# Moving a few sums and the gate weighting to other engines in a convolution plus mixture-of-experts kernel

## The chip, the core and the metric

The kernel runs on one core of one Trainium2 chip. Its time is the device time of one execution in microseconds (us), given as the median of several runs. The core has a matmul engine (TensorE, PE in the profile, with its weight loads as PEld) and three engines for elementwise work: VectorE (DVE), ScalarE (ACT) and GpSimd (POOL). SyncE (SP) issues nearly all DMA transfers; GpSimd issues the scatters with indices.

## The reference, cut to what matters

Each of 8 sequences of 5696 rows and 128 columns is convolved along its length with one common filter, and the result goes row by row through a mixture of experts, in which each row uses one expert of eight.

```python
Yf = np.fft.rfft(x, n=2 * S, axis=1) * np.fft.rfft(h, n=2 * S, axis=0)[None]
x = np.fft.irfft(Yf, n=2 * S, axis=1)[:, :S, :].reshape(B * S, D)

logits = x @ w_gate
expert_idx = np.argmax(logits, axis=1)
probs = softmax(logits)
gate_w = probs[np.arange(N), expert_idx]
for e in range(8):
    mask = expert_idx == e
    out[mask] = gate_w[mask, None] * (np.maximum(x[mask] @ w1[e], 0.0) @ w2[e])
```

Here B = 8, S = 5696, D = 128, N = B * S = 45568; w1 is 128x1024 and w2 1024x128 for each expert.

## The kernel before, in words

The long transform is split into a 119-point and a 48-point part. The batches go through it in three groups of 2, 3 and 3 (`SPLIT`). For each group there is an opening 119-point stage (`phase_a`), a 48-point stage (`phase_b`) and a closing 119-point stage with gating and sorting (`phase_c`). The opening stage of group 1 and of group 2 runs as a guest inside the closing stage of the group before.

**The 48-point stage.** In groups 1 and 2 it works on 120 items of 384 columns, software-pipelined by fixed lags. One item is: `forward` (matmuls into `xp`, L528), `product` (three VectorE instructions L540, L545 and L547 that read `xp` from PSUM and write `zt` and `xs`), `combine` (the sum `zt + xs`, L555), `inverse` (matmuls into `vp`, L564) and `save` (a ScalarE copy, L579). With the lags (1, 2, 4, 5), `combine` of an item is issued one item step after its `product`, and `inverse` two item steps after `combine`. `combine` runs on GpSimd, except that the first `ALONE[g]` items of group g run on VectorE; `ALONE` is (0, 0, 20), so that these are the first 20 items of group 2, in the third 48-point stage.

**The sort.** The closing stage finds an expert and a place for each row, and appends to the list `sorts`. `sort_one` takes one entry off the list and issues one scatter on GpSimd (L656) into the sorted rows `SR`, and a short filler instruction behind it (L650). The scatters are spread over the steps; what is left on the list when the closing stage ends is issued one by one in the next stage, one in each expert step, from inside `relu`.

**The experts.** Rows are read back in sorted tiles of 256 (182 of them). A tile has four steps; a step is `layer1` (matmuls L1164 into `mh`), `relu` on ScalarE (L1170) with the rest of the fp32 split on VectorE (L1172), and `layer2` (matmuls L1185 into `ma`) two steps later. In the step k = 2 TensorE also transposes the finished tile before it and the rows of the next one into one PSUM bank `mx` (L183); ScalarE and VectorE then cut the new rows in two parts (`xtb`, L1154 and L1155), ScalarE copies a finished sum out (`ot`, L1195), and `emit` multiplies the finished rows by their gate weights (L1203) and writes them over `xr`. `deliver` issues the scatters to `out` (L1240), two for each tile, on GpSimd. While a closing stage runs, finished tiles are stored to a staging buffer instead (`leave`, L1216), and read back later.

**The order.** Everything is issued in an order that is worked out when the program is built: `run` takes, of the streams that are alive, the one with the least planned time. So the interleaving of expert steps and transform work does not react to what happens on the chip. Each engine works its own queue in order. The experts run beside the second 48-point stage, both later closing stages and the third 48-point stage, and then alone to the end.

Of the kernel before, what the change touches and what calls it, by code (L numbers as in the profile page):

```python
# [17 lines left out]
AF = mybir.ActivationFunctionType  # L18
ALU = mybir.AluOpType
# [23 lines left out]
LD = 4  # L43
SHARES = (0.39, 0.93, 0.998, 0.84)
AHEAD = 2
ALONE = (0, 0, 20)
HALVES = ((12,), (8, 24), (24,))
STEP = 1420
MIX_A = (0.0, 0.45, 0.8)
# [28 lines left out]
def conv_moe(ctx: ExitStack, tc: tile.TileContext, I, out, B, S, D, E, F, split):  # L78
    nc = tc.nc
    P = 128  # L80
# [373 lines left out]
    def phase_b(gr, guest=None):  # L454
        g, cb, cw, nch, QB, QW = gr.g, gr.cb, gr.cw, gr.nch, gr.qb, gr.qw
# [95 lines left out]

        def combine(n):
            zt, xs = zts[n]
            eng = nc.vector if n < ALONE[g] else nc.gpsimd
            eng.tensor_tensor(out=zt, in0=zt, in1=xs, op=ALU.add)  # L555

        def inverse(n):
# [43 lines left out]
        for n in range(N + ds_ + 2 + (HOLD if QW == 1 else 0)):  # L601
# [21 lines left out]
            if 0 <= n - dc < N:  # L623
                combine(n - dc)
# [18 lines left out]
    sorts = []  # L643
# [556 lines left out]

    def emit(t, count):
        op, xr = obank.pop(t), rows.pop(t)
        nc.vector.tensor_tensor(  # L1203
            out=xr[:, :, :D], in0=op, in1=xr[:, :, D : D + 1].broadcast_to([P, 2, D]), op=ALU.mult
        )
        if state["defer"] and slot[0] < STAGED:
            leaving.append((count, STG[slot[0]], xr))
            slot[0] += 1
        else:
            pending.append((xr, 0))  # L1210
            pending.append((xr, 1))
# [52 lines left out]
    def pipeline(lo, hi):  # L1264
# [3 lines left out]
        while True:  # L1268
# [57 lines left out]
            if to is not None:  # L1326
                emit(to, len(hist))
# [141 lines left out]
```

## Time and profile before

| what | value |
|---|---|
| median of 3 runs | 2147.75 us (2144.11 to 2147.92) |
| the profiled execution's own time | 2146.88 us |
| its span, first to last instruction | 2145.2 us |
| busy share of the span: TensorE, VectorE, ScalarE, GpSimd | 96%, 73%, 51%, 59% |
| mean granted TensorE clock | 0.989 of full speed |

The busy share of an engine is a mean over stages that differ. A TensorE that is busy is not a TensorE at its best, since the ends of its matmuls are modelled. The shares for VectorE, ScalarE and GpSimd can be read as they stand.

### The profile page before, as it was taken

Reading aid. Unit: us, or ns where it says so; the run is one execution under the profiler, and the core shown is the slowest. Engines: PE = TensorE matmul, PEld = TensorE weight load, DVE = VectorE, ACT = ScalarE, POOL = GpSimd, SP = SyncE. Lnnn points to the kernel's source line nnn. Section 1 sums busy time; section 2 is a strip of 40 time slices with the busy share of each in tenths; the row PEclk is TensorE's granted clock in tenths of the full one; section 3 lists DMA queues with packets and bytes.
Section 4 is the critical chain, followed back from the end, with each engine's and each line's share of the span. In section 5 each row is a group of like instructions: output and inputs, shape, how many; then the busy total and the mean of one; then the engine's idle time right before and its main releaser. Section 6 shows DMA issues by size and latency. Waiting matters only on the chain.

```text
span 2145.2 us, 47047 instructions
## 1 busy us (share of the span) xinstructions
PE 2052.4 (96%) x14284; PEld 1763.9 (82%) x14284; DVE 1556.4 (73%) x3731; ACT 1104.5 (51%) x2359; POOL 1264.6 (59%) x1399
## 2 busy tenths in 40 slices
PE   7899899899999999989999999999999999999998
PEld 5788666666667988876777779999989999999998
DVE  3598856699987788879988885777765555555554
ACT  5688755233334666633443345655544444554544
POOL 5366547565653388882665661788876444444443
PEclk9999999999999999999999999999999999999999
DMA  9899999799997788767889886666645543444441
GB/s 340 291 301 325 320 395 366 213 278 279 272 279 234 288 273 296 264 198 218 250 249 248 243 246 228 212 209 211 199 149 186 170 139 108 142 138 143 143 144 34
DMA packets 236901, 494.39 MB, mean 230 GB/s; under 512 B 33553, under 2 KB 146446, under 8 KB 236647
## 3 DMA queue, kind: packets, MB, share of 16 engines
q1 hardware_dynamic: 212279, 443.06, 66.2%
q0 software_dynamic: 24368, 48.29, 6.9%
q8 instruction: 116, 1.90, 0.4%
q14 instruction: 138, 1.13, 0.2%
HBM read 598.31 MB, written 176.80 MB: 361 GB/s over the span
## 4 chain that ended last, share of the span: by engine, by line
PE 29%; issue 15%; POOL 13%; DMA 6%; DVE 6%; ACT 1%; SPq 1%; POOLq 1%; DVEq 0%; ACTq 0%
PE mh L1164 9%; PE ma L1185 8%; POOL out L1240 8%; POOL SR L656 3%; PE vp L564 3%; PE xp L528 3%; PE yp L742 2%; DMA SR<-rt,pi 2%; DMA wb<-WD 2%; POOL c_fcs L650 1%; PE mx L183 1%; DVE hs L1172 1%; PE pa L315 1%; PE tp L183 1%; DMA vq<-VU 1%
## 5 line engine op out<-in xcount | busy, mean ns | idle before, releaser
L1172 DVE SCALAR_TENSOR_TENSOR hs<-mh,hs 128x512 fp32r<-128x512 f32 x728 | 501.4, 691 | 371.6 <-ACT hs L1170 366.5
L1164 PE MATMUL mh<-xtb,wb 128*128 128x256 f32 x4368 | 686.0, 293 | 27.2 <-DMA wb<-WD 12.7
L1170 ACT ACTIVATE hs<-mh 128x512 fp32r<-128x512 f32 x728 | 435.7, 599 | 449.3 <-PE mh L1164 435.4
L1164 PEld LDWEIGHTS mh<-xtb,wb 128*128 128x128 f32 x4368 | 582.8, 189 | 95.3 <-issue 34.3
L1185 PE MATMUL ma<-hs,wb 128*128 128x256 f32 x4368 | 653.7, 285 | 7.3 <-DMA wb<-WD 7.3
L1185 PEld LDWEIGHTS ma<-hs,wb 128*128 128x128 f32 x4368 | 566.9, 190 | 8.7 <-DMA wb<-WD 8.7
L656 POOL DMA_INDIRECT SR<-rt,pi x384 | 402.8, 1049 | 196.3 <-issue 55.0
L1240 POOL DMA_INDIRECT out<-xr x250 | 243.8, 975 | 316.0 <-DVE xr L1203 257.7
L555 POOL TENSOR_TENSOR zt<-zt,xs 128x384 f32<-128x384 f32 (+1 forms) x280 | 298.3, 1075 | 115.3 <-DVE xs L547 86.9
L579 ACT COPY vt<-vp 96x384 f32<-96x384 f32 (+1 forms) x300 | 149.1, 497 | 349.2 <-PE vp L564 344.4
L564 PE MATMUL vp<-zt,mi 128*96 128x384 f32 (+1 forms) x720 | 259.2, 455 | 7.2 <-DVE xs L547 5.8
L528 PE MATMUL xp<-uq,mt 96*128 96x384 f32 (+1 forms) x720 | 258.7, 454 | 4.4 <-ACT vt L579 2.3
L540 DVE TENSOR_TENSOR zt<-xp,hh 128x384 f32<-128x384 f32 (+1 forms) x300 | 174.0, 580 | 54.6 <-PE xp L528 40.6
L564 PEld LDWEIGHTS vp<-zt,mi 128*96 128x96 f32 x720 | 113.3, 163 | 100.2 <-issue 52.1
L1240 POOL DMA_INDIRECT out<-xb x114 | 111.1, 975 | 135.3 <-ACT hs L1170 111.0
L547 DVE SCALAR_TENSOR_TENSOR xs<-xp,hh 64x384 f32<-64x384 f32 (+1 forms) x300 | 175.7, 586 | 6.1
L545 DVE TENSOR_TENSOR xs<-xp,hh 64x384 f32<-64x384 f32 (+1 forms) x300 | 173.2, 577 | 6.0
L315 PE MATMUL pa<-xc,fcr 120*128 120x512 f32 x576 | 166.8, 420 | 11.0 <-ACT xc L293 4.0
L528 PEld LDWEIGHTS xp<-uq,mt 96*128 96x128 f32 x720 | 121.7, 192 | 34.7 <-issue 13.1
L315 PEld LDWEIGHTS pa<-xc,fcr 120*128 120x128 f32 x576 | 101.5, 192 | 44.5 <-DVE rk L867 7.5
L650 POOL TENSOR_TENSOR c_fcs<-c_fcs 120x64 f32<-120x64 f32 (+1 forms) x288 | 125.9, 437 | 6.2
L742 PE MATMUL yp<-vr,gcr 120*120 120x384 f32 x576 | 117.5, 338 | 1.2 <-DVE vr L730 1.1
(137 smaller groups left out, 2275.6 us busy)
## 6 DMA issues: line engine op xcount, KB each, us to landing
wb<-WD SPq DMA_DIRECT2D x728, 512.0 KB
vq<-VU SPq DMA_DIRECT2D x64, 768.0 KB
VU<-ut SPq DMA_DIRECT2D x48, 768.0 KB
uq<-VU SPq DMA_DIRECT2D x60, 576.0 KB
VU<-vt SPq DMA_DIRECT2D x60, 576.0 KB
xt<-x SPq DMA_DIRECT2D x96, 256.0 KB
xr<-SR SPq DMA_DIRECT2D x182, 130.0 KB
hh<-HS SPq DMA_DIRECT2D x120, 192.0 KB
```

Source lines behind the costliest of these rows:

```text
L315: done = nc.tensor.matmul(banks[m], lhs, rhs, start=(k == 0), stop=(k == len(ops) - 1))
L528: nc.tensor.matmul(xj, mt[:, k0 + j, :], uc.rearrange("p (b d) -> p b d", d=D), start=True, stop=True)
L540: nc.vector.tensor_tensor(out=zt, in0=x3, in1=hv[:, 0].broadcast_to([P] + wide), op=ALU.mult)
L547: nc.vector.scalar_tensor_tensor(out=xs[to], in0=x3[at], scalar=-1.0, in1=him, op0=ALU.mult, op1=ALU.mult)
L555: eng.tensor_tensor(out=zt, in0=zt, in1=xs, op=ALU.add)
L564: nc.tensor.matmul(vp[:K2, j * cw : (j + 1) * cw].rearrange("p (b d) -> p b d", d=D), mi[:, k0 + j, :], zt.rearrange("p b (j d) -> p b j d ...
L656: s = nc.gpsimd.indirect_dma_start(out=SR[:, :], out_offset=IndirectOffsetOnAxis(ap=pi[:, b : b + 1], axis=0), in_=rt[:, b, :], in_offset= ...
L1164: nc.tensor.matmul(hp[:, u, :], wb[:, a, f, :], xt[:, b, :], start=(n == 0), stop=(n == 2))
L1170: done = nc.scalar.activation(hs[:, 0], hp, AF.Relu)
L1172: nc.vector.scalar_tensor_tensor(out=hs[:, 1], in0=hp, scalar=0.0, in1=hs[:, 0].bitcast(F32), op0=ALU.max, op1=ALU.subtract)
L1185: nc.tensor.matmul(accs[t], wb[:, a, f, :], hs[:, b, u, :], start=(k == 0 and u == 0 and n == 0), stop=(k == NPAIR - 1 and u == 1 and n == 2),
L1240: sc = nc.gpsimd.indirect_dma_start(out=out[:, :], out_offset=IndirectOffsetOnAxis(ap=xr[:, s, D + 1 : D + 2].bitcast(I32), axis=0), in_=x ...
```

## The change

Two edits. In `combine` the engine of the sum is no longer chosen by the number of the item: in group 2 it is VectorE as long as the list `sorts` is not empty at the time of issue, and GpSimd from then on. In `emit` the product of a 128x256 PSUM tile with the gate weights, one VectorE instruction, becomes two ScalarE activations of 128x128 with the gate weight as a scale for each partition.

```diff
-ALONE = (0, 0, 20)
...
         def combine(n):
             zt, xs = zts[n]
-            eng = nc.vector if n < ALONE[g] else nc.gpsimd
+            eng = nc.vector if g == 2 and sorts else nc.gpsimd
             eng.tensor_tensor(out=zt, in0=zt, in1=xs, op=ALU.add)
...
     def emit(t, count):
         op, xr = obank.pop(t), rows.pop(t)
-        nc.vector.tensor_tensor(
-            out=xr[:, :, :D], in0=op, in1=xr[:, :, D : D + 1].broadcast_to([P, 2, D]), op=ALU.mult
-        )
+        for s in range(2):
+            nc.scalar.activation(xr[:, s, :D], op[:, s], AF.Copy, scale=xr[:, s, D : D + 1])
```

## Rows read from the trace of the kernel before

**Rows 1.** Windows by stage: PE, PEld, DVE, ACT, POOL busy (count), clock, DMA share, GB/s.
```profile
415.00:655.00 240.00, 229.66 (x1098) 153.76 (x1096) 224.62 (x412) 83.33 (x186) 149.54 (x149) 0.99 1.02 272
655.00:955.00 300.00, 285.37 (x2137) 253.63 (x2137) 238.31 (x787) 183.60 (x423) 213.03 (x287) 0.98 0.79 261
955.00:1022.00 67.00, 61.96 (x350) 44.84 (x350) 64.65 (x131) 23.87 (x49) 20.24 (x27) 1.00 0.76 208
1022.00:1290.00 268.00, 261.91 (x1513) 201.34 (x1512) 232.15 (x426) 110.25 (x228) 163.62 (x165) 0.99 0.89 250
1290.00:1600.00 310.00, 300.87 (x2546) 286.31 (x2545) 224.24 (x752) 178.26 (x417) 219.20 (x285) 0.99 0.64 203
1600.00:2146.00 546.00, 535.70 (x4579) 534.60 (x4578) 301.97 (x528) 266.20 (x528) 259.37 (x275) 1.00 0.41 134
```

**Rows 2.** Waits of DVE in 415 to 655 us: total us, times, longest.
```profile
DVE zt L540 <- PE xp L528: 7.4, 7, 2.6
```

**Rows 3.** Windows 978 to 1022 us of all engines, columns as in rows 1.
```profile
978.00:1022.00 44.00, 40.83 (x224) 28.78 (x224) 42.52 (x79) 16.43 (x35) 8.69 (x9) 1.00 0.79 220
```

**Rows 4.** Waits of PE in 955 to 1022 us.
```profile
PE mh L1164 <- DVE hs L1172: 3.6, 5, 1.5
```

**Rows 5.** Instructions of line L555 on DVE over the span.
```profile
L555 DVE TENSOR_TENSOR zt<-zt,xs x20: 557/559/634, 963.4 to 1019.9; 128x384 f32<-128x384 f32 x20
```

**Rows 6.** Timeline of POOL: the last sort scatter and what follows.
```profile
975.09 1.01 POOL L656 DMA_INDIRECT SR<-rt,pi  x1 [1.69 <-ACT hs L1170]
...
986.22 0.99 POOL L1240 DMA_INDIRECT out<-xr  x1 [9.79 <-DVE xr L1203]
```

**Rows 7.** Timeline of ACT: the relu ahead of that scatter.
```profile
974.19 0.60 ACT L1170 ACTIVATE hs<-mh 128x512 fp32r<-128x512 f32 x1 [0.67 <-PE mh L1164]
```

**Rows 8.** Timeline of DVE in the early third 48-point stage.
```profile
975.22 0.56 DVE L555 TENSOR_TENSOR zt<-zt,xs 128x384 f32<-128x384 f32 x1
975.81 0.69 DVE L1172 SCALAR_TENSOR_TENSOR hs<-mh,hs 128x512 fp32r<-128x512 f32 x1
...
985.52 0.41 DVE L1203 TENSOR_TENSOR xr<-mx,xr 128x256 f32<-128x256 f32 x1
985.86 0.55 DVE L540 TENSOR_TENSOR zt<-xp,hh 128x384 f32<-128x384 f32 x1
```

**Rows 9.** Windows of line L540 (one instruction for each item): DVE busy (count).
```profile
978.00:1022.00 44.00, 8.23 (x15) 1.00 0.79 220
1022.00:1290.00 268.00, 54.02 (x98) 0.99 0.89 250
```

**Rows 10.** Windows of line L1203 by stage: DVE busy (count).
```profile
415.00:655.00 240.00, 5.40 (x13) 0.99 1.02 272
655.00:955.00 300.00, 8.30 (x20) 0.98 0.79 261
955.00:1022.00 67.00, 2.08 (x5) 1.00 0.76 208
1022.00:1290.00 268.00, 9.13 (x22) 0.99 0.89 250
1290.00:1600.00 310.00, 13.72 (x33) 0.99 0.64 203
1600.00:2146.00 546.00, 37.02 (x89) 1.00 0.41 134
```

**Rows 11.** Groups by line and shape: busy us, mean ns | idle before, releaser.
```profile
L555 POOL TENSOR_TENSOR zt<-zt,xs 128x384 f32<-128x384 f32 x220 | 222.2, 1020 | 81.2 <-DVE xs L547 69.9 <-PE vp L564 7.8 <-PE ma L1185 2.2
L1195 ACT COPY ot<-ma 128x256 f32<-128x256 f32 x182 | 67.8, 373 | 17.0 <-PE ma L1185 3.0
L797 ACT COPY lt<-tp 96x120 f32<-96x120 f32 x64 | 17.8, 279 | 0.0
```

**Rows 12.** Timeline of ACT: the relu behind an emit, with the idle time before it.
```profile
1434.26 0.60 ACT L1170 ACTIVATE hs<-mh 128x512 fp32r<-128x512 f32 x1 [0.58 <-PE mh L1164]
...
1705.28 0.60 ACT L1170 ACTIVATE hs<-mh 128x512 fp32r<-128x512 f32 x1 [1.00 <-PE mh L1164]
```

**Rows 13.** Waits of PE in 1290 to 1600 us.
```profile
PE mh L1164 <- DVE hs L1172: 6.3, 10, 3.0
PE mh L1164 <- ACT hs L1170: 1.4, 4, 0.5
```

## The prediction, made before the change was run

> **What bounds the kernel now.** I read the windows by stage first, since the kernel is a chain of stages with different limits [rows 1]. Expert work begins with the second 48-point stage, and nothing of the change acts before it. Five stretches remain, and one for the start of the third 48-point stage.
>
> In the second 48-point stage (415 to 655 us) VectorE is busy 224.62 of 240 us, and its list of waits holds one entry of size, 7.4 us for TensorE [rows 1, 2]. The reader is to see that VectorE hardly ever waits: it sets the pace. The same row shows the DMA engines at a share of 1.02, so a second limit lies close behind. At the start of the third 48-point stage VectorE is fuller still: 42.52 of 44 us in 978 to 1022 us [rows 3]. There TensorE waits for it, 3.6 us of it at the first layer for a free `mh` bank [rows 4]. After 1022 us TensorE is busy 261.91 of 268 us against VectorE's 232.15, and in the last stretch 535.70 of 546 against 301.97 [rows 1]. In both closing stages TensorE is busy 95% and 97% (285.37 of 300, 300.87 of 310). So an edit that frees VectorE is worth its time in the first stretch and at the start of the third 48-point stage, and little elsewhere.
>
> **Edit 1, the sums.** Today 20 sums run on VectorE, from 963.4 to 1019.9 us [rows 5]. In the new kernel they do so while the list of scatters is not empty. The order of issue is fixed when the program is built, so the trace of before tells how many that is. The last sort scatter starts at 975.09 us and is released by the relu that starts at 974.19 [rows 6, 7]. `relu` issues the activation, then the scatter, then the VectorE instruction L1172, which here is the one at 975.81; the sum at 975.22 stands ahead of it and is the fifth in the timeline of VectorE [rows 8]. So 5 sums stay and 15 move to GpSimd.
>
> On VectorE a sum takes from 975.22 to 975.81, 0.59 us from start to start [rows 8]; 15 of them are 8.9 us, out of a stretch of 44 us. On GpSimd a sum takes 1.02 us [rows 11], 15 of them 15.3 us. What hides them is that GpSimd works only 8.69 of these 44 us and stands idle for 9.79 us before the scatter at 986.22 [rows 3, 6]. The inverse matmuls come two item steps after the sum, 2 times 2.7 us by the pace below, so the longer sum has room. If that cover were gone (a sum behind a scatter to `out` that waits for its `xr`), an item would start up to one scatter, 0.99 us, later [rows 6]: that eats from the 5.4 us and not yet from TensorE. GpSimd's queue holds no transfer that this edit moves.
>
> With the sums gone VectorE needs about 34 of the 44 us and TensorE sets the pace. How fast is that? The stretch does 15 items in 44 us, 2.93 us for each; after 1022 us, where the sums already run on GpSimd, 98 items take 268 us, 2.73 us for each [rows 9]. The gain by pace is 15 times 0.20, 3.0 us. The other bound is TensorE's idle time from 955 to 1022 us, 67 less 61.96, 5.0 us [rows 1]. I take **4.0 us**, since the later pace contains waits for transfers.
>
> **Edit 2, the gate weighting.** It takes 182 instructions off VectorE. One costs 0.34 us from start to start (985.52 to 985.86) [rows 8], not its duration of 0.41. By stage there are 13, 20, 5, 22, 33 and 89 [rows 10].
>
> - *Second 48-point stage:* 13 times 0.34 is 4.4 us off the engine that sets the pace. The lower bound is nothing: the DMA share is 1.02 [rows 1], and transfers may not follow. VectorE would wait for them now if they were the limit, and waits 7.4 us in 240 [rows 2]. I take three quarters, **3.3 us**.
> - *Start of the third:* the 5 are inside the 4.0 us above, since TensorE's floor is reached anyhow.
> - *Rest of the third:* 22 times 0.34 is 7.5 us of VectorE time, but TensorE sets the pace, with 6.1 us idle in all [rows 1]. Bounds 0 to 2 us (a third of this idle time); I take **0.5 us**.
> - *Closing stages:* 53 of them. TensorE waits 6.3 us for VectorE's L1172 in the last one, 10 times [rows 13]; at most 10 times 0.34, 3.4 us, comes back. Against it stands ScalarE, below.
> - *Experts alone:* TensorE is full; nothing.
>
> ScalarE gets 364 activations of 128x128 from PSUM. The trace has none of that kind. The nearest rows bound it: a copy of 96x120 takes 0.279 us, one of 128x256 takes 0.373 us [rows 11]. So a tile costs 0.56 to 0.75 us; the low end is nearer by shape and I take it. That is 102 us on an engine that is half idle. What is queued behind it on ScalarE is the next relu, for which VectorE and then TensorE wait. In the experts-alone stretch ScalarE stands idle 1.00 us in that place, so both ends fit. In the closing stage shown it stands idle 0.58 us [rows 12]: 0.56 just fits, 0.75 runs 0.17 us over, 53 times 9.0 us at worst. With 3.4 us gained at one end and 9.0 lost at the other, I take **zero** for the closing stages.
>
> The Trainium skill (ScalarE: Activation LUTs, "What ACT_TABLE_LOAD costs") speaks against this edit: it says that a scale given as one value per partition makes an activation about 93 ns longer. By that rule an estimate from the copy's row is 0.74 us for a tile, beside the upper end above, and the sum of this change would lose up to those 9 us. No row here has such an operand in a form that could decide it.
>
> The scatter to `out` and the store to the staging buffer now wait for ScalarE instead of VectorE. In the first and third stretch ScalarE is the emptier engine (83.33 of 240 us), so `xr` is ready earlier, not later. At the very end one activation more lies on the path, 0.56 less 0.42: nothing that counts.
>
> **Sum.** 4.0 + 3.3 + 0.5 = 7.8 us. The profiled execution took 2146.88 us (its span 2145.2), which stands 0.9 us under the median of the runs; 2146.88 less 7.8 is **2139 us**.
>
> **Rivals.**
>
> *Transfers take it back.* The second 48-point stage has its DMA engines full [rows 1]; there the gain is 0, and at the start of the third stage half of it goes to waiting for spectra that arrive no sooner. That leaves about 2 us: 2145. For it: the share of 1.02. Against it: VectorE's few waits [rows 2].
>
> *ScalarE becomes the late engine* (the other side). Place: the closing stages, the relu behind an `emit`. ScalarE works 183.60 of 300 and 178.26 of 310 us there [rows 1], in bursts. If an `emit` falls into a burst, its whole 0.75 us goes to the relu, and TensorE waits for the bank. With 53 tiles at 0.25 us or more for each, 13 us are lost and the change turns slower than no change can be told from; at 0.4 us it is 21 us, less 7.8: 2160. For it: TensorE already waits 1.4 us for this relu [rows 13]. Against it: it waits 6.3 us for VectorE, which gets emptier.
>
> *VectorE held more than it seems.* All 4.4 and 5.0 us come, 2 in the rest of the third stage and 3.4 in the closing stages: 14.8 us, 2132.
>
> *The switch does not move the sums* (the list empties later than I read it): edit 2 alone remains. 5 times 0.34 at the start of the third stage, 3.3 and 0.5: 5.5 us, 2141. It falls inside the first case's range.
>
> **How the numbers follow.** A difference of 0.2%, 4.3 us, is about what a measurement of this kernel can tell from no change. My forecast, with a gain of 4.3 to 11 us, has a chance of 0.50, the fourth rival within it. The third has 0.13 and is faster too. Transfers that take it back have 0.23, within 0.2%. ScalarE late has 0.14, of which 0.11 end slower and 0.03 within 0.2%. Faster 0.63, same 0.26, slower 0.11. The range of 2133 to 2149 us leaves out the last rival's tail below and the slower cases above, some 0.15 together. The likeliest case alone is 2136 to 2143.
>
> **What would show it.** In the profile after: 5 sums on VectorE and 295 on GpSimd (in all three stages); no L1203 on VectorE; 364 activations of 0.28 to 0.37 us on ScalarE. The 120 items of the second 48-point stage end some 3 us earlier, and those of the third some 8 us earlier, in equal steps of one item near 2.73 us from its start on. VectorE shows idle time between 978 and 1022 us. The length of the closing stages and of the experts-alone stretch stays within 2 us; if the closing stages grow, with more waits of TensorE for L1170, ScalarE was the wrong home. If the second 48-point stage keeps its length while VectorE now waits for TensorE and transfers, the DMA rival holds.

## The result: 0.57% slower

Measured beside each other on one chip, 11 runs each, the kernel before took 2143.8 us (median; 2138.5 to 2147.92) and the changed kernel 2156.65 us (2146.99 to 2160.15). The ratio is 1.0057, with a 95% interval of 1.0041 to 1.0073: slower by 12.9 us, where 8 us of gain were predicted. It lies outside the predicted range of 2133 to 2149 us.

The profiled execution after took 2160.15 us (span 2158.4 us), with a mean granted clock of 0.987 against 0.989 before. That is 0.2%, too little for the loss. Lines of the new kernel behind L46, where `ALONE` stood, are one lower (L540 is L539, L1170 is L1169, L1172 is L1171), and two lower behind `emit` (L1240 is L1238); `emit` is L1203 again, now on ScalarE.

### The profile page after: what moved, and what is told of

The parts are those of the page before. It is cut to its first block, busy times and chain, and to the rows that moved or that the text cites. A ratio compares the mean times of both kernels' runs of the same rounds, so it can differ in the third digit from the quotient of the medians.

```text
span 2158.4 us, 47892 instructions
## 1 busy us (share of the span) xinstructions
PE 2060.6 (95%) x14284; PEld 1768.3 (82%) x14284; DVE 1492.9 (69%) x3535; ACT 1200.5 (56%) x2723; POOL 1279.9 (59%) x1413
## 3 DMA queue, kind: packets, MB, share of 16 engines
q14 instruction: 144, 1.18, 0.2%
## 4 chain that ended last, share of the span: by engine, by line
PE 66%; DMA 12%; DVE 9%; issue 4%; ACT 4%; POOL 4%; SPq 1%; POOLq 0%; DVEq 0%; ACTq 0%
PE mh L1163 19%; PE ma L1184 19%; PE vp L563 8%; PE xp L527 7%; DMA SR<-rt,pi 4%; DMA wb<-WD 4%; PE yp L741 3%; PE mx L182 3%; PE pa L314 3%; POOL SR L655 2%; DVE hs L1171 1%; DMA vq<-VU 1%; PE tp L182 1%; DVE xs L546 1%; DVE xs L544 1%
## 5 line engine op out<-in xcount | busy, mean ns | idle before, releaser
L1171 DVE SCALAR_TENSOR_TENSOR hs<-mh,hs 128x512 fp32r<-128x512 f32 x728 | 500.9, 690 | 417.2 <-ACT hs L1169 411.7
L1169 ACT ACTIVATE hs<-mh 128x512 fp32r<-128x512 f32 x728 | 435.9, 600 | 279.4 <-PE mh L1163 279.0
L1238 POOL DMA_INDIRECT out<-xr x250 | 244.3, 977 | 305.9 <-ACT xr L1203 262.8
L554 POOL TENSOR_TENSOR zt<-zt,xs 128x384 f32<-128x384 f32 (+1 forms) x294 | 311.9, 1072 | 105.8 <-DVE xs L546 71.3
L578 ACT COPY vt<-vp 96x384 f32<-96x384 f32 (+1 forms) x300 | 148.5, 496 | 267.4 <-PE vp L563 260.9
L539 DVE TENSOR_TENSOR zt<-xp,hh 128x384 f32<-128x384 f32 (+1 forms) x300 | 174.2, 581 | 59.4 <-PE xp L527 45.1
L1203 ACT ACTIVATE xr<-mx,xr 128x128 f32<-128x128 f32 x360 | 112.7, 364 | 183.9 <-DVE xtb L1154 183.9
L1238 POOL DMA_INDIRECT out<-xb x114 | 111.2, 976 | 129.8 <-ACT hs L1169 107.1
L649 POOL TENSOR_TENSOR c_fcs<-c_fcs 120x64 f32<-120x64 f32 (+1 forms) x288 | 130.8, 454 | 6.7
```

Source lines behind the costliest of these rows:

```text
L1169: done = nc.scalar.activation(hs[:, 0], hp, AF.Relu)
L1171: nc.vector.scalar_tensor_tensor(out=hs[:, 1], in0=hp, scalar=0.0, in1=hs[:, 0].bitcast(F32), op0=ALU.max, op1=ALU.subtract)
L1238: sc = nc.gpsimd.indirect_dma_start(out=out[:, :], out_offset=IndirectOffsetOnAxis(ap=xr[:, s, D + 1 : D + 2].bitcast(I32), axis=0), in_=x ...
```

## The profile after

A stage's length is best read from one instruction that runs all through it: VectorE's first product for a 48-point stage (one for each item), the matmuls into `yp` for a closing stage. These are the instructions of that line in the kernel before (minimum, median and maximum ns, then the first and the last start in us): second 48-point stage, closing stage of group 1, third 48-point stage, closing stage of group 2.

```profile
L540 DVE TENSOR_TENSOR zt<-xp,hh x120: 545/557/560, 414.8 to 669.4; 128x384 f32<-128x384 f32 x120
L742 PE MATMUL yp<-vr,gcr x288: 333/337/437, 688.4 to 920.1; 120*120 120x384 f32 x144
L540 DVE TENSOR_TENSOR zt<-xp,hh x120: 545/548/560, 959.3 to 1282.2; 128x384 f32<-128x384 f32 x120
L742 PE MATMUL yp<-vr,gcr x288: 334/337/434, 1310.5 to 1563.3; 120*120 120x384 f32 x144
```

And the same four in the kernel after:

```profile
L539 DVE TENSOR_TENSOR zt<-xp,hh x120: 545/557/559, 418.9 to 671.2; 128x384 f32<-128x384 f32 x120
L741 PE MATMUL yp<-vr,gcr x288: 333/337/439, 690.6 to 930.6; 120*120 120x384 f32 x144
L539 DVE TENSOR_TENSOR zt<-xp,hh x120: 545/548/560, 968.8 to 1284.0; 128x384 f32<-128x384 f32 x120
L741 PE MATMUL yp<-vr,gcr x288: 331/337/436, 1312.9 to 1574.2; 120*120 120x384 f32 x144
```

Last start less first start, stage by stage:

| stretch | before | after | difference | predicted |
|---|---|---|---|---|
| second 48-point stage | 254.6 | 252.3 | −2.3 | −3.3 |
| closing stage of group 1 | 231.7 | 240.0 | +8.3 | 0 |
| third 48-point stage | 322.9 | 315.2 | −7.7 | −4.5 |
| closing stage of group 2 | 252.8 | 261.3 | +8.5 | 0 |

Both 48-point stages get shorter, by 10.0 us together against the 7.8 that were predicted; whether the 2.3 us of the second one are more than chance is taken up below. The two closing stages give back 16.8 us, where the prediction had zero. The rest of the 13.2 us between the two spans: 4.1 us had been lost before the first item (414.8 to 418.9), where nothing of the change acts, and 2.3 us come behind the last closing stage; the gaps between the stages cancel.

The windows after that answer to rows 1 and 3 (busy time of PE, PEld, DVE, ACT and POOL with counts, clock, DMA share, GB/s):

```profile
655.00:955.00 300.00, 285.20 (x2119) 249.00 (x2117) 229.36 (x757) 194.59 (x464) 208.43 (x276) 1.00 0.76 254
978.00:1022.00 44.00, 43.27 (x244) 32.14 (x245) 41.36 (x76) 19.17 (x44) 24.01 (x25) 1.00 0.85 225
1290.00:1600.00 310.00, 296.79 (x2507) 278.76 (x2505) 207.58 (x695) 194.58 (x478) 212.88 (x278) 1.00 0.65 204
```

At the start of the third 48-point stage (978 to 1022 us) TensorE is busy 43.27 of 44 us against 40.83 before [rows 3]. In the last closing stage everything but ScalarE does less in the same 310 us: VectorE 207.58 against 224.24, and TensorE 296.79 us with 2507 matmuls against 300.87 with 2546 [rows 1]. No engine became full that was not: ScalarE is busy 194.58 of 310. Taken from the first to the last start of the `yp` matmuls, TensorE does the same 1722 and 2116 matmuls in both kernels, at a granted clock of 1.00 in both, and stands idle 9.3 and 9.9 us where it stood idle 4.3 and 4.4 us before. These are 10.6 of the 16.8 us; the rest lies in its busy time, whose ends are modelled. A TensorE that waits more while no other engine is full must be held up by one that stands still at the wrong moment.

The groups by line name the place (busy us, mean ns | idle time of the engine just before, and what ended it):

```profile
L1203 ACT ACTIVATE xr<-mx,xr 128x128 f32<-128x128 f32 x360 | 112.7, 364 | 183.9 <-DVE xtb L1154 183.9
```

Ahead of the new instruction ScalarE stands idle for 183.9 us, all of it ended by L1154 of VectorE. That is more than the 112.7 us that the instruction works. L1154 is the second of the two instructions that cut the new rows into `xtb`; it reads the other half of the same PSUM tile `mx`. It takes nothing from `emit` and gives it nothing: of `mx` both only read. But the program as built makes the second reader wait for the first. While VectorE did both, they stood in one queue and there was no such wait.

One tile in the last closing stage, in the timeline of the kernel after (start, duration, engine, line, operation, tiles; in brackets the idle time before it and what ended that):

```profile
1439.34 0.36 ACT L1153 CAST xtb<-mx 128x256 fp32r<-128x256 f32 x1
1439.46 0.96 PE L1163 MATMUL mh<-xtb,wb 128*128 128x256 f32 x6
...
1440.58 0.68 DVE L1171 SCALAR_TENSOR_TENSOR hs<-mh,hs 128x512 fp32r<-128x512 f32 x1
...
1441.17 0.41 DVE L1154 TENSOR_TENSOR xtb<-mx,xtb 128x256 fp32r<-128x256 f32 x1
...
1441.62 0.63 ACT L1203 ACTIVATE xr<-mx,xr 128x128 f32<-128x128 f32 x2 [1.91 <-DVE xtb L1154]
...
1442.14 0.60 ACT L1169 ACTIVATE hs<-mh 128x512 fp32r<-128x512 f32 x1
...
1442.77 0.69 DVE L1171 SCALAR_TENSOR_TENSOR hs<-mh,hs 128x512 fp32r<-128x512 f32 x1 [1.18 <-ACT hs L1169]
```

ScalarE ends its part of the cut at 1439.70 and is free. VectorE works a chain of small gating instructions (lines 750 to 872) until 1440.6, then a relu rest, and starts L1154 only at 1441.17. Until that is done the pair of activations stands at the head of ScalarE's queue, 1.91 us long. The next relu is behind it. Its matmuls ran from 1439.46 to about 1440.4; it starts at 1442.14. VectorE in turn waits 1.18 us for that relu. Both engines are idle in turn, each for the other.

The waits after in 1290 to 1610 us (total us, times, longest):

```profile
ACT xr L1203 <- DVE xtb L1154: 32.4, 34, 1.9
DVE vr L729 <- ACT vr L728: 21.3, 24, 1.4
PE mh L1163 <- DVE hs L1171: 12.5, 13, 2.8
```

The first line is 0.95 us for each of 34 tiles (between 655 and 955 us it is 25.3 us for 21 tiles, 1.20 each). The second is another ScalarE instruction that comes late behind it; in the list of before it had 6.2 us, 13 times. The third is TensorE's wait for a free `mh` bank: 12.5 us, 13 times, against 6.3 us, 10 times [rows 13]. Within the closing stage itself, from the first `yp` matmul to the last, it is 8.9 us against 2.3.

The first closing stage is held up at another place. Its waits for `mh` stay below 1 us in both kernels; TensorE's idle time there is spread over small waits for other tiles, and what grows beside it is VectorE's wait for ScalarE's late `vr`, from 13.8 us (16 times) to 22.8 us (23 times).

## The experiments

Two theories, and a third against both:

- **Wait:** `emit` on ScalarE waits for VectorE's read of `mx`, and the relu behind it is late. Free of the wait, the same work costs nothing.
- **Work:** 0.63 us more in bursts on ScalarE make the relu late. This is the rival that the prediction had named.
- **Sums:** the edit of the sums is what lengthens the closing stages.

The kernels ran in three sets, each on a chip of its own with its own runs of the kernel before. Times compare within a set. Stage lengths are last less first start of the same lines as above, in each kernel's profiled execution, in us.

| set | kernel | median us | before, same chip | ratio [95% interval] | closing 1 | third 48-point | closing 2 | closings together |
|---|---|---|---|---|---|---|---|---|
| 1 | e1_sums_only | 2178.04 | 2184.28 | 0.9974 [0.9956, 0.9992] | 235.3 | 315.6 | 252.4 | 487.7 |
| 1 | e2_gate_only | 2207.11 | 2184.28 | 1.0106 [1.0084, 1.0129] | 241.2 | 319.1 | 261.6 | 502.8 |
| 1 | e3_emit_first | 2177.98 | 2184.28 | 0.9977 [0.9958, 0.9995] | 236.9 | 313.7 | 252.7 | 489.6 |
| 1 | e4_vector_in_closing | 2189.26 | 2184.28 | 1.0012 [0.9993, 1.003] | 232.5 | 317.5 | 251.7 | 484.2 |
| 2 | before_again | 2196.26 (one run) | 2199.79 | | 236.6 | 321.5 | 251.9 | 488.5 |
| 2 | after_again | 2217.25 | 2199.79 | 1.0073 [1.0046, 1.01] | 245.6 | 313.3 | 262.1 | 507.7 |
| 2 | e5_scalar_work_alone | 2196.19 | 2199.79 | 0.9989 [0.997, 1.0009] | 239.0 | 318.3 | 253.7 | 492.7 |
| 2 | e6_wait_alone | 2209.69 | 2199.79 | 1.0043 [1.0021, 1.0065] | 243.8 | 313.6 | 259.4 | 503.2 |
| 3 | e7_scalar_in_48 | 2134.35 | 2144.61 | 0.9955 [0.9938, 0.9971] | 231.7 | 313.3 | 252.8 | 484.5 |
| 3 | e1_repeat | 2138.13 | 2144.61 | 0.9977 [0.9958, 0.9996] | 231.5 | 315.0 | 252.8 | 484.3 |
| 3 | e8_sums_all_gpsimd | 2136.25 | 2144.61 | 0.9971 [0.9954, 0.9989] | 231.7 | 315.9 | 252.7 | 484.4 |

The closings together are the number to read. They fall into two groups: 484.2 to 492.7 us where ScalarE has no wait for VectorE's cut ahead of its next relu in these stages, and 501.3 (the changed kernel above) to 507.7 us where it has. TensorE's wait for VectorE at `mh` within the second closing stage falls into the same two groups: 1.7 to 2.8 us in nine kernels' profiles, and 7.4 to 9.0 us in the four of after, after_again, e2 and e6.

### Each edit alone: e1_sums_only and e2_gate_only

e1 is the changed kernel with the gate product back on VectorE; e2 is the kernel before with the gate product on ScalarE.

```diff
 e1_sums_only, against the changed kernel
-        for s in range(2):
-            nc.scalar.activation(xr[:, s, :D], op[:, s], AF.Copy, scale=xr[:, s, D : D + 1])
+        nc.vector.tensor_tensor(
+            out=xr[:, :, :D], in0=op, in1=xr[:, :, D : D + 1].broadcast_to([P, 2, D]), op=ALU.mult
+        )
 e2_gate_only, against the kernel before
-        nc.vector.tensor_tensor(
-            out=xr[:, :, :D], in0=op, in1=xr[:, :, D : D + 1].broadcast_to([P, 2, D]), op=ALU.mult
-        )
+        for s in range(2):
+            nc.scalar.activation(xr[:, s, :D], op[:, s], AF.Copy, scale=xr[:, s, D : D + 1])
```

> Edit 1 alone: the sums move, the gate weighting stays on VectorE. If the loss comes from the gate weighting on ScalarE (both of the theories below), this kernel is faster than before by 4 to 7 us, all of it at the start of the third 48-point stage (matmul by matmul, the changed kernel gained 7.0 us there and lost 18 us in the two closing stages). If the loss comes from the sums on GpSimd, it is slower than before by some 10 us.

> Edit 2 alone: 20 sums on VectorE as before, the gate weighting on ScalarE. If the gate weighting is what costs: closing stages longer by 9 us each, 3 us back in the second 48-point stage and 3 at the start and in the rest of the third, so 10 to 15 us slower than before. If the sums are what costs: 3 to 6 us faster than before.

The sums alone gain 0.26%, the gate alone loses 1.06%. The closing stages of e2, and the group of its `emit`:

```profile
L742 PE MATMUL yp<-vr,gcr x288: 333/337/437, 708.0 to 949.2; 120*120 120x384 f32 x144
L742 PE MATMUL yp<-vr,gcr x288: 333/338/434, 1339.5 to 1601.1; 120*120 120x384 f32 x144
L1204 ACT ACTIVATE xr<-mx,xr 128x128 f32<-128x128 f32 x360 | 113.0, 365 | 185.6 <-DVE xtb L1155 176.1 <-DVE hs L1172 7.9 <-issue 1.7
```

The same idle time stands there without the sums being touched, and the closings take 502.8 us against 487.7 in e1. So the sums are not what lengthens the closing stages; the theory "sums" falls. The loss of e2, 22.8 us at the medians, is larger than the 10 to 15 us expected of it: 15.1 us lie in the closing stages, and 7.4 us behind the last of them, of which more below.

### The same work without the wait: e3_emit_first

The changed kernel with `emit` issued ahead of `turned_in`, the function that holds L1153 and L1154. Then `emit` is the first reader of the bank and has only TensorE to wait for. The number of instructions stays the same on every engine.

```diff
+            if to is not None:
+                emit(to, len(hist))
             if ti is not None:
                 turned_in(ti)
                 turned += 1
             if old and old[1] == NPAIR - 1:
                 drain(old[0])
-            if to is not None:
-                emit(to, len(hist))
             deliver(done)
```

> Both edits, but in the order of issue the gate weighting stands ahead of the two instructions that split the new rows (L1153, L1154), so that it no longer waits for VectorE to have read the shared PSUM bank. Theory 'wait' (ScalarE stands still until VectorE has read the bank, and the next relu with it): the idle time of ScalarE before L1203, 183.9 us in the changed kernel, falls to near nothing, the closing stages lose most of the 18 us, and the kernel is 4 to 10 us faster than before. Theory 'work' (0.73 us of ScalarE time for a tile is what the relu behind it cannot bear): the closing stages stay 14 us or more longer than before, and the kernel is 5 us or more slower than before.

Its closing stages and the group of its `emit`:

```profile
L741 PE MATMUL yp<-vr,gcr x288: 333/337/437, 707.5 to 944.4; 120*120 120x384 f32 x144
L741 PE MATMUL yp<-vr,gcr x288: 334/337/439, 1328.5 to 1581.2; 120*120 120x384 f32 x144
L1203 ACT ACTIVATE xr<-mx,xr 128x128 f32<-128x128 f32 x360 | 112.1, 369 | 1.3 <-PE mx L182 1.3
```

The idle time ahead of `emit` falls from 183.9 to 1.3 us, the closings take 489.6 us, and the kernel is 0.23% faster than before instead of slower. ScalarE works as much as in the changed kernel, 112.1 us in this place. But one order of issue was changed along with it, so the next two kernels part the work from the wait on one base.

### The work alone and the wait alone: e5_scalar_work_alone and e6_wait_alone

Both start from e1_sums_only, where VectorE does the gate product. e5 adds two activations with the same kind of scale behind it, on data in SBUF and into a scratch tile: work on ScalarE, but no read of `mx`. e6 adds one copy of a single column of `xtb` ahead of `emit`: next to no work, but it waits for L1154. What they write is not used.

```diff
 e5_scalar_work_alone, against e1_sums_only
+        for s in range(2):
+            nc.scalar.activation(fcs[:, 1], ident[:MP], AF.Copy, scale=xr[:MP, s, D : D + 1])
 e6_wait_alone, against e1_sums_only
             if to is not None:
+                if ti is not None:
+                    nc.scalar.copy(fcs[:, 1, :1], xts[ti][:MP, 1, :1].bitcast(F32))
                 emit(to, len(hist))
```

> The sums move as in edit 1 and the gate weighting stays on VectorE; ScalarE gets two more activations of 120x128 for each tile behind it, from SBUF to an unused buffer, which nothing reads: the work of edit 2 without the wait on the shared PSUM bank. Theory 'wait': the closing stages and the experts-alone stretch stay near those of the kernel with edit 1 alone, and the time within 5 us of it, that is 1 to 6 us faster than before. Theory 'work': closing stages longer by 14 us or more, slower than before by 8 us or more.

> The sums move as in edit 1 and the gate weighting stays on VectorE; ScalarE gets one copy of 120x1 for each tile that reads what VectorE's split of the new rows (L1154) writes: the wait of edit 2 nearly without its work. Theory 'wait': most of the loss is there, closing stages longer by 8 to 18 us than with edit 1 alone, and the kernel slower than before by 3 to 12 us. Theory 'work': as fast as edit 1 alone, 4 to 7 us faster than before.

The groups by line of the added instructions, first of e5, then of e6:

```profile
L1206 ACT ACTIVATE c_fcs<-ident,xr 120x128 f32<-120x128 f32 x364 | 148.5, 408 | 5.9
```

```profile
L1327 ACT COPY c_fcs<-xtb 120x1 f32<-120x1 f32 x180 | 34.5, 192 | 178.9 <-DVE xtb L1154 170.4 <-DVE hs L1171 7.7 <-issue 0.8
```

e5 puts 148.5 us on ScalarE, more than the 112.7 of the changed kernel, and stays within its interval of the kernel before (0.9989). e6 puts 34.5 us on it with 178.9 us of idle time ahead, and is 0.43% slower. The closing stages of e6:

```profile
L741 PE MATMUL yp<-vr,gcr x288: 333/337/522, 709.5 to 953.3; 120*120 120x384 f32 x144
L741 PE MATMUL yp<-vr,gcr x288: 334/337/439, 1343.2 to 1602.6; 120*120 120x384 f32 x144
```

They take 503.2 us together, e5's 492.7, and before_again's, on the same chip, 488.5. The wait makes 14.7 of after_again's 19.2 us (507.7 less 488.5). The work adds 4.2 in this profile (492.7 less 488.5); profiles without the wait on one chip differ by as much (484.2 to 489.6 in set 1), so that nothing is shown for the work, and a small cost isn't ruled out.

### The pair again on another chip: before_again and after_again

Both kernels unchanged, to see the pair's stages a second time.

> The kernel before once more, for a profile from the same chip as the experiments beside it. It should take what the runs of before beside it take.

> The changed kernel once more on the chip of the experiments. Slower than before by 10 to 16 us, with some 18 us more in the two closing stages. In the first set of experiments the kernel with the gate weighting alone also lost 7 us in the stretch where the experts run alone, since the copy of a finished sum behind the late relu came late; on such a chip the changed kernel loses these 7 us too.

It was slower by 0.73%. The closings differ by 19.2 us (16.8 in the first pair), the third 48-point stage by −8.2 (−7.7), the second by −2.5 (−2.3). New against the first pair is a loss in the last stretch, in which experts run alone: TensorE's weight loads for the transposes wait for ScalarE's copy `ot`. The waits of 1750 to 2100 us, first before_again, then after_again:

```profile
PEld mx L183 <- ACT ot L1195: 0.9, 5, 0.2
```

```profile
PEld mx L182 <- ACT ot L1194: 10.8, 47, 0.4
```

From the last `yp` matmul to the end of the span after_again took 606.9 us and before_again 596.8, 10.1 us more. In the first pair it was only 2.3 us more. TensorE's matmuls in 1750 to 2100 us say the same: 3000 before and 2999 after in the first pair; 2944 to 2965 in the kernels of sets 1 and 2 without the wait there (before_again, e1, e3, e5), and 2901 to 2919 in those with it (after_again, e2, e4, e6). So what the wait costs in this stretch was not the same in the first pair as in these two sets; why is open.

### VectorE only in the closing stages: e4_vector_in_closing

The changed kernel with `emit` on VectorE where a closing stage runs (`state["defer"]`), on ScalarE elsewhere.

```diff
-        for s in range(2):
-            nc.scalar.activation(xr[:, s, :D], op[:, s], AF.Copy, scale=xr[:, s, D : D + 1])
+        if state["defer"]:
+            nc.vector.tensor_tensor(
+                out=xr[:, :, :D], in0=op, in1=xr[:, :, D : D + 1].broadcast_to([P, 2, D]), op=ALU.mult
+            )
+        else:
+            for s in range(2):
+                nc.scalar.activation(xr[:, s, :D], op[:, s], AF.Copy, scale=xr[:, s, D : D + 1])
```

> Both edits, but while finished tiles are stored for later (the closing stages) the gate weighting stays on VectorE. Both theories put the loss into the closing stages: there the lengths go back to those of before, the 48-point stages keep their gains, and the kernel is 8 to 12 us faster than before. If the loss of 18 us there is not due to the gate weighting (chance, transfers), it stays.

A miss as a version: 1.0012, no gain, where 8 to 12 us had been expected. The closing stages came back as expected (484.2 us). But it keeps the wait where experts run alone, and there the same loss shows (603.9 us behind the last `yp` matmul, 596.1 in e1), in the waits of 1750 to 2100 us:

```profile
PEld mx L182 <- ACT ot L1194: 7.3, 31, 0.5
```

In e1, on the same chip, this wait is 1.4 us, 8 times. The profiled execution of e4 also reached its first item at 446.1 us, the three others of that set at 437.7 to 439.5, and nothing that was edited acts before it; why is open.

### ScalarE in the 48-point stages alone: e7_scalar_in_48, with e1_repeat and e8_sums_all_gpsimd

e7 lets ScalarE do the gate product only while a 48-point stage of group 1 or 2 runs, and there ahead of `turned_in`; elsewhere VectorE does it as before. e1_repeat is e1_sums_only again beside it. e8 is e1 with every sum on GpSimd.

```diff
 e7_scalar_in_48, against the changed kernel (state["mid"] is set in the loop of the 48-point stage)
-        for s in range(2):
-            nc.scalar.activation(xr[:, s, :D], op[:, s], AF.Copy, scale=xr[:, s, D : D + 1])
+        if state["mid"]:
+            for s in range(2):
+                nc.scalar.activation(xr[:, s, :D], op[:, s], AF.Copy, scale=xr[:, s, D : D + 1])
+        else:
+            nc.vector.tensor_tensor(
+                out=xr[:, :, :D], in0=op, in1=xr[:, :, D : D + 1].broadcast_to([P, 2, D]), op=ALU.mult
+            )
...
+            if to is not None and state["mid"]:
+                emit(to, len(hist))
             if ti is not None:
                 turned_in(ti)
...
-            if to is not None:
+            if to is not None and to in obank:
                 emit(to, len(hist))
 e8_sums_all_gpsimd, against e1_sums_only
-            eng = nc.vector if g == 2 and sorts else nc.gpsimd
+            eng = nc.gpsimd
```

> Both edits, but the gate weighting is on ScalarE only while a 48-point stage of group 1 or 2 runs, and there ahead of the split of the new rows, so that it does not wait for VectorE; elsewhere it stays on VectorE. Theory 'wait': the closing stages and the experts-alone stretch are as with edit 1 alone, the two 48-point stages a few us shorter, and the kernel 6 to 10 us faster than before, 1 to 4 us faster than edit 1 alone. If VectorE does not set the pace in the second 48-point stage after all (transfers do), it is no faster than edit 1 alone.

> Edit 1 alone once more, beside the two others: 4 to 7 us faster than before, as in the first set.

> Edit 1 taken further: all sums on GpSimd, none on VectorE, the gate weighting on VectorE. The five sums that then stand behind the last sort scatters free 3 us of VectorE at most, but wait for GpSimd, which has one scatter and one filler per step there. Within 3 us of edit 1 alone, so still 2 to 8 us faster than before. If GpSimd's scatters matter as the condition of edit 1 supposes, it is slower than edit 1 alone by more than 3 us.

e7 has the lowest ratio of all: 2134.35 us, 0.45% under the kernel before and, by two ratios from different sets, about 1% under the changed one. Its closing stage of group 1, third 48-point stage, and closing stage of group 2:

```profile
L742 PE MATMUL yp<-vr,gcr x288: 333/337/437, 690.4 to 922.1; 120*120 120x384 f32 x144
L539 DVE TENSOR_TENSOR zt<-xp,hh x120: 545/548/560, 959.0 to 1272.3; 128x384 f32<-128x384 f32 x120
L742 PE MATMUL yp<-vr,gcr x288: 334/337/434, 1300.9 to 1553.7; 120*120 120x384 f32 x144
```

The closings are those of the kernel before in the first pair (484.5 us both), and the third 48-point stage is 9.6 us shorter than there. e1_repeat gains 0.23%, e8 0.29%. Their intervals overlap with e7's, and e7's second 48-point stage is not the shorter one that was expected (254.8 us, against 250.9 in e1_repeat), so what the gate product on ScalarE adds in the 48-point stages isn't shown. e8 and e1_repeat don't differ either: the condition on the scatter list does no more than all sums on GpSimd.

## Why the prediction was wrong

**The step that failed** is "I take **zero** for the closing stages", with its bound of "0.75 runs 0.17 us over, 53 times 9.0 us at worst". The bound came from comparing the length of the activations with ScalarE's idle time ahead of a relu, as if `emit` started as soon as ScalarE came to it. It starts when VectorE has read the other half of `mx`, about 1 us later (1.20 and 0.95 us for a tile in the windows of the two closing stages). Measured: +16.8 and +19.2 us in two pairs, beyond even the 9.0 us that were put as the worst. That this wait is the cause is shown from both sides: e3 keeps the work and loses the wait (489.6 us), e6 has the wait and hardly any work (503.2), e5 the work and no wait (492.7). The prediction asked what stands behind the moved instruction in its new queue, but not for which other engine's read it would have to wait there.

**The rival "ScalarE becomes the late engine"** came true in its place (the relu behind an `emit`, as far as the last closing stage shows it) and nearly in its price: it gave 13 us from 0.25 us for each of 53 tiles, and 16.8 over 53 is 0.32 us. Its mechanism was another: not bursts of work (e5 has them) but a wait. It had 0.11 for slower; [rows 13], TensorE's waits for VectorE, had been read as the case against it, and in the last closing stage these very waits doubled.

**Edit 1, the sums,** was right, and mis-sized a little. It was given 4.0 us; alone it gains 0.26% and 0.23% by the ratios, 5.7 us of 2184.28 and 4.9 us of 2144.61 (the medians differ by 6.2 and 6.5 us). The ten profiles with the sums moved have third 48-point stages of 313.3 to 318.3 us, the three without 319.1 to 322.9. Six sums stayed on VectorE, not five, as the instructions of that line show:

```profile
L554 DVE TENSOR_TENSOR zt<-zt,xs x6: 558/559/559, 972.8 to 987.2; 128x384 f32<-128x384 f32 x6
```

The sixth could be read in the kernel before. The relu at 974.19, which released the last sort scatter, was paired with the L1172 at 975.81, but that one belongs to the relu ahead of it. There are two `mh` banks, and the first layer at 976.55 waits for the bank of the relu before:

```profile
976.55 0.96 PE L1164 MATMUL mh<-xtb,wb 128*128 128x256 f32 x6 [0.40 <-DVE hs L1172]
```

So the L1172 of 974.19 is the next one, at 978.72, and the sum at 978.13 stands ahead of it too. With 14 moved instead of 15 the working hardly changes. What was too small is the gain in pace. From 18.7 us behind the stage's first item, where [rows 3] begin, the kernel before does 15 items in 44 us; e1_repeat, with this edit alone, does 17 (975.6 to 1019.6 us), 2.59 us each where 2.73 was expected, and 15 times the 0.34 us between 2.93 and 2.59 is 5.1 us. TensorE is busy 43.70 of these 44 us and sets the pace, as predicted. VectorE doesn't fall to 34 us: it is busy 40.31, since more items pass.

**Edit 2 in the second 48-point stage,** 3.3 us: the two pairs show −2.3 and −2.5, but over all profiles the stage takes 249.7 to 254.6 us with the gate product on VectorE and 248.5 to 254.8 us with it on ScalarE. Whether the 13 instructions are worth anything there stays open. The rival "transfers take it back" isn't refuted for this stage.

**The size of the activation.** The bounds were 0.56 and 0.75 us for a tile, and 0.56 was taken. One takes 0.364 us, close to the upper end of 0.373 for each, but the two overlap: 0.63 us from start to end in the timeline above, near the middle. The Trainium skill (ScalarE: Activation LUTs, "What ACT_TABLE_LOAD costs") says that a scale given per partition adds about 93 ns, and that back-to-back activations overlap by about 93 ns. The trace agrees with both: an estimate from the copy in rows 11 is 0.279 plus 0.093, 0.372 us, against the 0.364 measured, and one for the pair is twice 0.364 less 0.093, 0.635 us, against 0.63. The prediction had drawn on the first half of that rule alone.

**"`xr` is ready earlier, not later"** was wrong, for the reason of the failed step: however empty ScalarE is, its `emit` waits for VectorE's read of the new rows. One tile of the second 48-point stage, first before, then after:

```profile
443.03 0.41 DVE L1155 TENSOR_TENSOR xtb<-mx,xtb 128x256 fp32r<-128x256 f32 x1
443.36 0.41 DVE L1203 TENSOR_TENSOR xr<-mx,xr 128x256 f32<-128x256 f32 x1
```

```profile
447.14 0.41 DVE L1154 TENSOR_TENSOR xtb<-mx,xtb 128x256 fp32r<-128x256 f32 x1
447.59 0.63 ACT L1203 ACTIVATE xr<-mx,xr 128x128 f32<-128x128 f32 x2 [0.91 <-DVE xtb L1154]
```

From the start of that read to the end of `emit` it was 0.74 us and is 1.08, and so in each tile of both 48-point stages within 0.02 us. This delay of 0.3 us cost nothing that could be seen: GpSimd has room. Its idle time ahead of the scatters of `xr` was 316.0 us before and is 305.9 us now.

**What stays open.** Whether the chip needs a wait between two reads of one PSUM tile wasn't tried; the experiments moved the reader instead of taking the wait away, so nothing here says that it may be left out. Behind the last closing stage the loss is 2.3 us in one pair and 10.1 in the other; in e2 it is 7.4 us against e1, beside 15.1 us in the closings (502.8 less 487.7), of the 29.1 us between their medians.

## What to carry to other kernels

An instruction that moves to an emptier engine takes its dependences with it, and some of them become waits that were none while both ends stood in one queue: look for every other engine that touches the same PSUM tile, and ask when that engine gets there. What such a wait costs is not its own lateness but that of whatever stands behind it in the new queue; issuing the moved instruction ahead of the other reader cost nothing that could be seen here, and the kernel was 0.23% faster than before instead of 0.57% slower (each against the kernel before on its own chip). The gain that is shown, that of the sums, came where VectorE had been full (42.52 of 44 us), so place a move by stage, not by the busy share of the whole span.

## What the runs showed of the hardware that was not expected

The unchanged kernel had medians of 2143.8, 2184.28, 2199.79 and 2144.61 us in the four groups of runs, a spread of 2.6%, several times the effect measured here. About half of it lies ahead of the first item of the second 48-point stage: before reached that item at 414.8 us and before_again at 441.3, of the 49 us between their spans, with a mean granted clock of 0.98 and 0.94 in the first 400 us; why is open. An activation of 120x128 with a scale per partition took 0.408 us from SBUF (e5), one of 128x128 from PSUM 0.364 us.
